# A gated linear attention and a feed-forward block in one kernel: a new order table for all five engines

## The chip, the core and the metric

The kernel runs on one core of a Trainium2 chip. The core has five engines that run side by side, each working through its own instructions in order: TensorE (PE in the profile: matrix products, PEld being the load of their stationary operand), VectorE (DVE), ScalarE (ACT), GpSimd (POOL) and SyncE (SP). DMA transfers are started by SP, ACT or POOL, each with a queue of its own, and are carried out by 16 DMA engines. Engines wait for one another on semaphores. Results of PE go to PSUM, which the kernel handles as eight banks; everything else is in SBUF.

The metric is the device time of one execution in microseconds (us). The kernel before took 189.69 us, the median of three runs (189.52 to 190.71).

## The reference

The first half is a recurrence over 768 steps for 4 batches of 8 heads with 48 features each, with a complex decay `a` whose magnitude is capped at 0.999. The second half normalises the 384 features of each token, multiplies by a gain, and applies two matrices with a ReLU between them, plus the residual.

```python
mag = np.sqrt(a_re * a_re + a_im * a_im)
scale = np.minimum(mag, 0.999) / (mag + 1e-06)
a_re_n, a_im_n = (a_re * scale, a_im * scale)
for t in range(S):                                   # S = 768
    new_re = ar * S_re - ai * S_im                   # ar, ai: a_re_n, a_im_n at t
    new_im = ar * S_im + ai * S_re
    S_re, S_im = (new_re + kv, new_im)               # kv: outer product of k[t] and v[t]
    y[:, :, t] = np.einsum('bhd,bhde->bhe', q[:, :, t], S_re)
...
xn = (x - mu) / np.sqrt(var + 1e-06) * g_ln          # x: y with the heads side by side
ch = np.maximum(xn @ w_ch1, 0.0) @ w_ch2             # 384 -> 1536 -> 384
return (x + ch).astype(np.float32)
```

## The kernel before

The 768 steps of a batch are cut into six chunks of 128, and two chunks make a pair, so that there are 12 pairs (P = 0 to 11, three for each batch) and 24 chunks (n = 2P and 2P+1). The recurrence is done by chunks: the logarithm of the magnitude and the angle of `a` are summed along the steps by matrix products with a triangular matrix, and q and k are scaled by the exponentials of these sums and turned by sine and cosine. Then a chunk is a masked product of q, k and v, plus q times a state that is carried from chunk to chunk. The feed-forward block of a pair follows when both of its chunks have their output.

Every step is a named operation (`g.add`, lines 160 to 162). For pair P the names are, in the order of their dependence:

- `are`, `aim`, `q`, `k`, `vf`: loads; `ln`, `iv`, `r`, `r2`, `u`, `l`, `lc`: logarithm of the magnitude and the ratio of the two parts of `a` (lines 454 to 475); `dec`: the sums of the logarithms on PE (line 483); `en`, `e`: their exponentials on ACT (line 487); `th`, `ph`, `car`, `sin`, `qt` or `abs`, `cos`: angle, its sums on PE (line 508), the carry to the next pair, sine and cosine.
- `ke`, `qe`, `ks`, `qs`: the scaled and turned k and q, all of them `tensor_tensor` operations recorded at line 295, on DVE or POOL.
- `kT`, `qT` (eight transposes each on PE, line 614) with `ksT`, `qsT` (the copy out of PSUM by DVE or ACT, lines 290 and 292); or `ksT`, `qsT` on SP alone, which is a DMA that transposes (line 619) and needs no PE.
- `am`, `atm`: the product of k and q and its mask (lines 637 and 295); `gm`, `G`: the carried state; `y`, `x`: output of the chunk and its copy; `bn`, `rstd`: mean and variance, and the reciprocal root, on POOL or ACT; `xtr`, `xT`: the transpose of x, three on PE (line 708) and a copy.
- `mm1.P.g.part`: the first matrix, six products of 256 columns each (line 742); `relu.P.g` (lines 759 on ACT, 761 on DVE); `mm2.n.g`: the second matrix, four products of 384 columns (line 774), for the last chunk in two halves of 192 columns; `oa` and `ot`: scaling and residual, as one DVE operation (line 790) or one on ACT and one on POOL (lines 780 and 787); `st`: the store (line 797).
- `wl`: loads of the two weight matrices through POOL's queue, with a change of type; `wp`, `wc`: gain and mean folded into the first matrix (lines 390 and 394).
- `warm.i`: fill-ins on PE (line 807), products whose result nobody reads; `tab`: loads of ACT's function tables (line 812).

What runs where and in which order is written out by hand in one string, `PLAN`. A token `relu.4.1:A4` says: operation, engine (P, A, V, G, S for PE, ACT, DVE, POOL, SP) and, where the result passes through PSUM, the bank. `@x` after a POOL operation makes its first instruction wait for the last one of `x`. `Graph.run` goes through the tokens once and emits them; each engine gets its operations in the order of the string, and the waits between engines come from the tiles and banks that the operations share:

```python
for op in steps:
    for n in op.needs:
        assert n in done or n not in planned, (op.name, n)
    ...
    op.emit()
    made[op.name] = list(traced[n_traced:])
    done.add(op.name)
for op in steps:
    if op.behind:
        tc.add_manual_dep(made[op.name][0], made[op.behind][-1].name, info,
                          reason="turns at the shared port")
```

Two things follow that the steps of the prediction use. A DMA whose letter is `A` is started by ACT's own instruction stream, in its place between the activations; one with `S` stands in SP's stream (`ring`, line 285). And a DMA's start can have to wait: the program counts DMAs with a handful of semaphores, which are used again and again, so that a start can stand until an earlier DMA, of another queue even, has landed.

Of the kernel before, what the change touches and what calls it, by code (L numbers as in the profile page):

```python
# [39 lines left out]
aim.0.0:A tab.log.0:A aim.0.1:A ue:G are.0.0:S are.0.1:S pad.e.1:G uth:V pickf:V one:G warm.0:P0 pad.ks.0:G warm.1:P0  # L40
warm.2:P0 pick:G warm.3:P0 are.1.0:S warm.4:P0 warm.5:P0 warm.6:P0 k.0.1:S ln.0.0:A warm.7:P0 car0.1:G warm.8:P0
cmean:G iv.0.0:A warm.9:P0 ident:G warm.10:P0 warm.11:P0 r.0.0:V warm.12:P0 warm.13:P0 warm.14:P0 aim.1.0:S warm.15:P0
warm.16:P0 warm.17:P0 ln.0.1:A warm.18:P0 warm.19:P0 r2.0.0:A warm.20:P0 k.0.0:S warm.21:P0 warm.22:P0 warm.23:P0
warm.24:P0 u.0.0:A warm.25:P0 warm.26:P0 warm.27:P0 warm.28:P0 iv.0.1:A warm.29:P0 l.0.0:V warm.30:P0 are.2.0:S
warm.31:P0 warm.32:P0 ln.1.0:A warm.33:P0 warm.34:P0 r.0.1:G warm.35:P0 lc.0.0:V warm.36:P0 warm.37:P0 aim.2.0:S
warm.38:P0 warm.39:P0 warm.40:P0 iv.1.0:A warm.41:P0 warm.42:P0 pad.ks.1:G warm.43:P0 warm.44:P0 warm.45:P0 warm.46:P0
warm.47:P0 zdec:G r2.0.1:A warm.48:P0 pad.e.0:G warm.49:P0 pad.qs.0:G warm.50:P0 q.0.1:S warm.51:P0 warm.52:P0 u.0.1:A
warm.53:P0 warm.54:P0 r.1.0:V warm.55:P0 dec.0.0:P0 warm.56:P1 warm.57:P1 q.1.0:S e.0.0:A0 warm.58:P1 warm.59:P1
warm.60:P1 r2.1.0:V warm.61:P1 en.0.0:A0 warm.62:P1 warm.63:P1 warm.64:P1 l.0.1:V warm.65:P1 u.1.0:A warm.66:P1
warm.67:P1 warm.68:P1 warm.69:P1 lc.0.1:V warm.70:P1 are.3.0:S warm.71:P1 warm.72:P1 warm.73:P1 ln.2.0:A warm.74:P1  # L50
l.1.0:V warm.75:P1 warm.76:P1 warm.77:P1 warm.78:P1 dec.0.1:P6 q.1.1:S warm.79:P0 warm.80:P0 lc.1.0:V en.0.1:A6
# [792 lines left out]
```

## Time and profile before

| what | value |
|---|---|
| median of three runs | 189.69 us |
| the profiled execution's own time | 190.44 us |
| its span, first to last instruction | 188.7 us |
| PE busy | 177.6 us (94%) |
| ACT busy | 159.0 us (84%) |
| DVE busy | 156.6 us (83%) |
| POOL busy | 105.0 us (56%) |
| packets of SP's DMA queue | 72.8% of 16 engines' span |
| packets of ACT's DMA queue | 17.4% |
| packets of POOL's DMA queue | 8.2% |

Busy times are of the profiled execution, and the 1.74 us between its span and its own time lie around the program. Products on PE overlap, so that their durations add up to more than they cost in sequence; what a group costs is read from starts that follow one another, or from the chain of waits, where overlaps are taken out. Starting a DMA, waiting on a semaphore and branching are not counted as busy.

### The profile page before, as it was taken

What the parts mean: (1) busy time and instruction counts of PE and PEld (TensorE: products, weight loads), DVE (VectorE), ACT (ScalarE), POOL (GpSimd) and SP (SyncE); (2) the same over time, 40 slices, a digit from 0 to 9 for tenths busy, and PEclk for the clock granted to TensorE, in tenths of its full rate; (3) what the DMA queues carried; (4) which work ended last, traced back from release to release, by engine and by line L of the source; (5) the groups of instructions that cost most, each with busy time, mean ns of one, the idle gap of its engine ahead of it and who ended that gap; (6) DMA issues with size and microseconds to landing.
All of it is one profiled execution on the core that took longest, in us unless ns stands there. A gap on an engine that the chain in (4) does not pass through costs nothing.

```text
span 188.7 us, 5157 instructions
## 1 busy us (share of the span) xinstructions
PE 177.6 (94%) x2045; PEld 136.7 (72%) x2045; DVE 156.6 (83%) x287; ACT 159.0 (84%) x224; POOL 105.0 (56%) x124
## 2 busy tenths in 40 slices
PE   5999789999999999999959999999999999998991
PEld 3897565888657888766747687878867777786781
DVE  2677999999999999999996988998989867775532
ACT  3969899999999999899959999998999979762340
POOL 7409233579187899080549392348784963940130
PEclk9999999999999999999999999999999999999998
DMA  6999999999969998889999999999799979994032
GB/s 162 287 258 179 220 213 203 222 221 193 238 119 300 184 227 232 156 194 237 161 269 210 191 239 235 281 225 201 137 170 250 216 124 178 248 218 148 5 125 83
DMA packets 133080, 37.57 MB, mean 199 GB/s; under 512 B 127168, under 2 KB 133056, under 8 KB 133056
## 3 DMA queue, kind: packets, MB, share of 16 engines
q1 hardware_dynamic: 107760, 27.21, 72.8%
q10 hardware_dynamic: 22512, 7.67, 17.4%
q0 software_dynamic: 2784, 2.36, 8.2%
q8 instruction: 16, 0.26, 0.6%
q14 instruction: 8, 0.07, 0.1%
HBM read 28.31 MB, written 4.72 MB: 175 GB/s over the span
## 4 chain that ended last, share of the span: by engine, by line
PE 57%; DVE 17%; DMA 7%; SPq 6%; ACT 3%; issue 3%; POOL 3%; ACTq 1%; DVEq 0%; POOLq 0%
PE banks L774 21%; PE banks L742 15%; PE banks L637 4%; DMA w2b<-in_moe_w_ch_dram 4%; SPq L451 4%; PE banks L508 3%; PE banks L614 3%; DVE w1b L394 3%; DMA q<-in_q_dram 3%; PE banks L483 2%; DVE atm L295 2%; SPq L410 2%; PE banks L687 2%; PE banks L690 2%; PE banks L665 2%
## 5 line engine op out<-in xcount | busy, mean ns | idle before, releaser
L774 PE MATMUL banks<-w2b,h 128*128 128x384 bf16 (+1 forms) x300 | 55.5, 319 | 0.7 <-ACT h L759 0.5
L742 PE MATMUL banks<-xT,w1b 128*128 128x256 bf16 x432 | 50.7, 272 | 0.2 <-ACT sh L551 0.2
L742 PEld LDWEIGHTS <-w1b 128*128 128x128 bf16 x432 | 41.4, 98 | 6.3 <-DVE xT L292 0.4
L774 PEld LDWEIGHTS <-h 128*128 128x128 bf16 x300 | 26.7, 97 | 13.6 <-ACT h L759 1.0
L295 DVE TENSOR_TENSOR atm<-banks,mask 128x1024 bf16<-128x1024 f32 x24 | 28.9, 1220 | 3.0 <-PE banks L637 2.2
L759 ACT ACTIVATE h<-banks 128x1024 bf16<-128x1024 f32 (+1 forms) x26 | 25.6, 1008 | 3.9 <-DVE ks L295 2.3
L812 ACT ACT_TABLE_LOAD x19 | 24.4, 1283 | 1.8 <-PEq L828 1.3
L295 POOL TENSOR_TENSOR ke<-k,en 128x384 bf16<-128x384 f32 x17 | 15.4, 916 | 14.9 <-ACT en L487 4.7
L807 PE MATMUL banks<-u_e 128*128 128x256 f16 x134 | 18.2, 293 | 2.2 <-POOL u_e L324 2.2
L787 POOL TENSOR_TENSOR ot<-ot,x 128x384 f32<-128x384 f32 x13 | 12.1, 936 | 14.6 <-ACT ot L780 12.4
L295 POOL TENSOR_TENSOR r<-aim,are 128x768 f16<-128x768 f32 (+1 forms) x8 | 13.7, 1715 | 10.8 <-DVE w1b L394 4.1
L295 POOL TENSOR_TENSOR qs<-qe,trig 128x768 bf16<-128x768 bf16 x8 | 13.0, 1640 | 8.4 <-DVE w1b L394 5.4
L807 PEld LDWEIGHTS <-u_e 128*128 128x128 f16 x134 | 13.9, 105 | 4.8 <-POOL u_e L324 1.9
L637 PE MATMUL banks<-qsT,ksT 128*128 128x128 bf16 x192 | 14.5, 219 | 2.5 <-DVE stats L700 1.9
L637 PEld LDWEIGHTS <-ksT 128*128 128x128 bf16 x192 | 12.0, 97 | 4.6 <-issue 2.3
L761 DVE TENSOR_SCALAR h<-banks 128x1024 bf16<-128x1024 f32 (+1 forms) x11 | 12.8, 1167 | 2.8 <-PE banks L742 2.8
L295 POOL TENSOR_TENSOR qe<-q,e 128x384 bf16<-128x384 f32 x12 | 10.9, 916 | 6.8 <-DVE r L295 3.6
L472 DVE SCALAR_TENSOR_TENSOR l<-r,w 128x768 f16<-128x768 f16 (+1 forms) x13 | 12.7, 977 | 1.7 <-ACT r L468 1.7
L700 DVE BATCH_NORM_STATS2 stats<-x 128x6 f32<-128x384 bf16 x24 | 13.1, 546 | 0.1
L454 ACT ACTIVATE w<-are 128x768 f32<-128x768 f32 (+1 forms) x13 | 10.4, 801 | 2.0 <-DMA are<-in_a_re_dram 1.5
L687 PE MATMUL banks<-v,atm 128*128 128x48 bf16 x192 | 11.9, 183 | 0.0
L687 PEld LDWEIGHTS <-atm 128*128 128x128 bf16 x192 | 10.7, 96 | 1.1 <-DVE atm L295 0.4
(101 smaller groups left out, 379.3 us busy)
## 6 DMA issues: line engine op xcount, KB each, us to landing
k<-in_k_dram SPq DMA_DIRECT2D x24, 192.0 KB, 5.0
q<-in_q_dram SPq DMA_DIRECT2D x24, 192.0 KB, 4.5
are<-in_a_re_dram SPq DMA_DIRECT2D x11, 384.0 KB, 5.4
aim<-in_a_im_dram SPq DMA_DIRECT2D x11, 384.0 KB, 4.9
out_dram<-ot ACTq DMA_DIRECT2D x19, 192.0 KB, 3.4
vf<-in_v_dram ACTq DMA_DIRECT2D x18, 192.0 KB, 4.7
w1b<-in_moe_w_ch_dram POOLq DMA_DIRECT2D x3, 384.0 KB, 7.0
vf<-in_v_dram SPq DMA_DIRECT2D x6, 192.0 KB, 6.6
```

Source lines behind the costliest of these rows:

```text
L295: {"DVE": nc.vector, "POOL": nc.gpsimd}[eng(name)].tensor_tensor(**kw)
L472: nc.vector.scalar_tensor_tensor(out=S_("l"), in0=S_("r2"), scalar=0.5, in1=S_("w"), op0=ALU.mult, op1=ALU.add)
L637: nc.tensor.matmul(ps[:, h], lhsT=T("ksT", n)[:, h], rhs=T("qsT", n)[:, h], start=True, stop=True)
L687: nc.tensor.matmul(ps[:, h], lhsT=T("atm", n)[:, h], rhs=T("v", P)[:, c, h], start=True, stop=nfirst)
L700: nc.vector.bn_stats(out=T("stats", n), in_=T("x", n))
L742: nc.tensor.matmul(ps[:, jj], lhsT=w1b[:, dc, ts(gi * JG + jj, C)], rhs=T("xT", P)[:, dc].rearrange("p c t -> p (c t)"), start=(dc == 0), ...
L759: act(out=dst, in_=src, func=AF.Relu)
L761: nc.vector.tensor_scalar(out=dst, in0=src, scalar1=0.0, scalar2=None, op0=ALU.max)
L774: nc.tensor.matmul(bank(own)[:, 0:w], lhsT=T("h", P)[:, j, ts(c, C)], rhs=w2b[:, j, es], start=(j == 0), stop=(j == NJ - 1))
L787: nc.gpsimd.tensor_tensor(out=T("ot", n)[:, es], in0=T("ot", n)[:, es], in1=T("x", n)[:, es], op=ALU.add)
L807: g.add(f"warm.{i}", lambda i=i: nc.tensor.matmul(bank(f"warm.{i}")[:, 0:256], lhsT=u_e[:, 0, 0], rhs=u_e[:, 1].rearrange("p j t -> p (j t ...
L812: g.add(f"tab.{nm}.{i}", lambda tab=tab: nc.scalar.preload_act_table_set(tab))
```

## The change

The string `PLAN` is replaced as a whole, and the number of fill-ins goes from 134 to 124. The code of the operations is the same. Compared by operation:

- From PE to DMA: `qT.6` (eight transposes) and `xtr.11` (three) are gone; `qsT.6` and `xT.11` are transposing DMAs on SP.
- To POOL: 5 more `ks`, 4 more `ke`, 4 more `v`, 2 more `qe`, 1 more `qs`; from POOL 5 `ot`, 1 `r`, 1 `r2`, 1 `rstd`.
- To ACT: 4 more `xT`, 2 more `x`, 2 more `r2`, 2 more `car`, 1 more `ksT`, 1 more `rstd`; from ACT 5 `oa`, 4 `v`, 3 `G`, 3 `abs`, 2 `relu`.
- DVE gets 5 `ot`, 3 `G`, 3 `abs`, 2 `relu`, 1 `r` and gives 5 `ks`, 5 `xT`, 4 `ke`, 2 `x`, 2 `qe`, 2 `car` and one each of `qs`, `ksT`, `qsT` and `r2`.
- DMA starts: 9 `vf` and 10 `st` move from ACT's stream to SP's, one `are` from SP's to ACT's. ACT's stream starts 21 DMAs where it started 39.
- The order on every engine, the banks, and the POOL operations with an `@` are new.

Of the diff (all of `PLAN`, 104 lines each way), the lines that the prediction speaks of:

```diff
-aim.0.0:A tab.log.0:A aim.0.1:A ue:G are.0.0:S are.0.1:S pad.e.1:G uth:V pickf:V one:G warm.0:P0 pad.ks.0:G warm.1:P0
...
-warm.31:P0 warm.32:P0 ln.1.0:A warm.33:P0 warm.34:P0 r.0.1:G warm.35:P0 lc.0.0:V warm.36:P0 warm.37:P0 aim.2.0:S
...
-lc.7.0:V aim.8.0:S v.5:V mm1.4.2.1:P2 relu.4.1:A4 st.3:A relu.4.0:V6 qs.6.0.1:G@v.5 kT.11:P1 relu.4.2:A2 aim.9.0:S
-dec.7.0:P4 ksT.11:V1 k.7.1:S mm2.8.0:P6 e.7.0:A4 ke.6.0.0:V am.11:P2 en.7.0:A4 ks.6.0.0:V mm2.8.1:P6 q.7.1:S bn.9:V
...
-relu.10.0:V2 mm1.10.2.0:P4 ot.19:G mm1.10.1.0:P6 relu.10.2:A4 st.18:A st.15:A st.12:A gm.22:P1 mm1.10.1.1:P6 rstd.10:A
...
-relu.11.2.0:V4 mm2.22.1:P6 mm2.23.1.0:P7 mm2.23.0.1:P0 mm2.23.1.1:P0 mm2.22.2:P6 ot.22:V6 mm2.23.2.0:P7 mm2.23.2.1:P0
-st.22:S ot.23.0:V7 st.23.0:S ot.23.1:V0 st.23.1:S
+pickf:V ue:G aim.0.0:A are.0.1:A cmean:G pick:G aim.0.1:A are.0.0:S tab.log.0:A ln.0.0:A iv.0.0:A r.0.0:V gln:S
+are.1.0:S q.0.1:S ln.0.1:A iv.0.1:A r2.0.0:A u.0.0:A r.0.1:V r2.0.1:G ident:G car0.1:G uth:V l.0.0:V lc.0.0:V
+aim.1.0:S pad.ks.0:G@lc.0.0 are.2.0:S aim.2.0:S pad.e.0:G ln.1.0:A iv.1.0:A r.1.0:V u.0.1:A one:G k.0.0:S l.0.1:V
...
+mm2.9.0:P7 ks.6.0.1:V am.11:P2 st.4:S mm2.8.0:P6 mm2.8.1:P6 r.8.0:G@qs.6.0.1 st.3:S e.7.0:A4 ke.7.0.0:G am.10:P0
...
+rstd.4:G@r2.8.0 mm2.9.1:P7 ke.7.0.1:G ot.8:V6 xtr.10:P2 ph.9.0:P0 xT.11:S are.10.0:S r2.9.0:V mm2.9.2:P7 xT.10:A2
...
+rstd.10:G@qs.11.0.0 ot.21:V1 mm1.11.2.0:P2 st.17:A mm1.11.2.1:P2 ot.20:V0 st.20:S ot.18:G@v.11 relu.11.0:A4
+mm2.23.0.1:P0 mm2.22.0:P5 relu.11.1:V6 rstd.11:G relu.11.2.0:V2 st.18:S mm2.22.1:P5 relu.11.2.1:V2 mm2.22.2:P5
+ot.22:V5 st.22:S mm2.23.1.1:P0 mm2.23.2.1:P0 ot.23.1:V0 st.21:A st.23.1:S mm2.23.0.0:P6 mm2.23.1.0:P6 mm2.23.2.0:P6
+ot.23.0:V6 st.23.0:A
...
-    for i in range(134):
+    for i in range(124):
```

In the new string the order of tokens of different engines says nothing of time, since all 43 first fill-ins, for instance, stand behind operations that they don't wait for; only the order within an engine counts.

192 lines of the change are left out of this document (95 added, 97 removed).

## The prediction

> **What bounds the kernel now.** I read the busy shares first, then the busy time by stretch, then the chain of waits, and then the order of time around each place where PE stands still.
>
> ```profile
> span 188.7 us, 5157 instructions
> PE 177.6 (94%) x2045; PEld 136.7 (72%) x2045; DVE 156.6 (83%) x287; ACT 159.0 (84%) x224; POOL 105.0 (56%) x124
> PEclk9999999999999999999999999999999999999998
> L807 PE MATMUL banks<-u_e 128*128 128x256 f16 x134 | 18.2, 293 | 2.2 <-POOL u_e L324 2.2
> ```
>
> PE is busy for 94% of the span, and its clock is granted in full. But 18.2 us of that are fill-ins (line 807), so the share doesn't say that PE is the bound at the start. So the span is cut where the first product with the first weight matrix begins (36.84 us, pair 0), and where pair 5's begins (107.45 us):
>
> ```profile
> 36.84 0.82 PE L742 MATMUL banks<-xT,w1b 128*128 128x256 bf16 x6
> 107.45 0.82 PE L742 MATMUL banks<-xT,w1b 128*128 128x256 bf16 x6
> 36.84:107.45 70.61, 68.56 (x817) 51.73 (x813) 66.95 (x122) 65.83 (x88) 45.92 (x47) 1.00 1.09 211
> 107.45:184.40 76.95, 76.27 (x897) 59.70 (x896) 59.37 (x108) 61.79 (x90) 42.28 (x40) 1.00 0.92 184
> 0.00:36.30 36.30, 31.65 (x324) 24.45 (x325) 28.46 (x56) 30.85 (x48) 16.27 (x38) 1.00 1.03 219
> 36.30:106.62 70.32, 68.27 (x821) 51.95 (x819) 66.64 (x122) 65.54 (x86) 46.46 (x47) 1.00 1.07 211
> ```
>
> The columns are the stretch, its length, and then busy time of PE, PEld, DVE, ACT and POOL. Between the two marks PE is idle for 70.61 - 68.56 = 2.05 us, and from 107.45 to 184.40 for 0.68 us. So after 36.84 us PE sets the time, with DVE and ACT close behind: the last two rows end at ACT's copies `xT.0` (36.30) and just ahead of `xT.10` (106.62), and between these ACT is idle for 70.32 - 65.54 = 4.78 us, DVE for 3.68 us. Nearly all of PE's 2.05 us is one stop:
>
> ```profile
> 94.57 1.00 ACT L759 ACTIVATE h<-banks 128x1024 bf16<-128x1024 f32 x1
> 97.45 0.36 ACTq L797 DMA_DIRECT2D out_dram<-ot  x1
> 97.92 1.02 ACT L759 ACTIVATE h<-banks 128x1024 bf16<-128x1024 f32 x1 [2.34 <-DVE ks L295]
> 98.99 0.61 PE L637 MATMUL banks<-qsT,ksT 128*128 128x128 bf16 x8 [1.91 <-DVE stats L700]
> ```
>
> The chain of waits names DVE here. But PE's product (`am.11`, banks 2 and 3) starts 0.05 us after the ReLU on ACT that empties these banks (`relu.4.2`, 97.92 + 1.02), and that ReLU starts right behind a store's start on ACT (`st.3`, 97.45 + 0.36). ACT stood 2.34 us with a store at the head of its stream. The second stop, and the end:
>
> ```profile
> 168.74 2.28 ACTq L797 DMA_DIRECT2D out_dram<-ot  x3
> 171.06 0.20 ACT L724 ACTIVATE rstd<-mv 128x2 f32<-128x2 f32 x1 [1.36 <-DVE G L292]
> 172.47 0.82 PE L774 MATMUL banks<-w2b,h 128*128 128x384 bf16 x4 [0.53 <-ACT h L759]
> 184.39 1.27 DVE L790 SCALAR_TENSOR_TENSOR ot<-banks,rstd,x 128x384 f32<-128x384 f32 x3 [2.17 <-PE banks L774]
> 185.04 1.30 SPq L797 DMA_DIRECT2D out_dram<-ot  x3
> ```
>
> Again three stores on ACT, a late `rstd.10`, a late ReLU, and 0.53 us of PE. Behind the last product come three DVE operations and three stores one after the other.
>
> **The change part by part.** The sum is made against the span of 188.7 us. The profiled execution took 190.44 us, the median is 189.69; differences are carried over as they are.
>
> Start, up to `xT.0`. PE fills time with fill-ins here, so ACT's stream decides.
>
> ```profile
> 7.55 2.12 DVE L475 TENSOR_SCALAR l<-l 128x384 f16<-128x384 f16 x1
> 11.63 0.26 DVE L475 TENSOR_SCALAR l<-l 128x384 f16<-128x384 f16 x1
> 7.42 1.00 POOL L295 TENSOR_TENSOR r<-aim,are 128x384 f16<-128x384 f32 x1 [2.76 <-ACT are L456]
> 10.84 0.49 ACT L487 ACTIVATE e<-banks 128x384 bf16<-128x384 f32 x1 [0.93 <-PE banks L483]
> 13.68 0.49 ACT L487 ACTIVATE en<-banks 128x384 bf16<-128x384 f32 x1 [0.51 <-PE banks L483]
> 21.12 0.87 ACT L534 ACTIVATE trig<-banks 128x384 bf16<-128x384 int16 x2 [0.58 <-DVE car L529]
> L464 ACT ACTIVATE r<-r 128x768 f16<-128x768 f16 x2 | 1.7, 840 | 0.2 <-issue 0.2
> L526 ACT ACTIVATE car<-banks 32x384 f16<-32x384 int16 x4 | 1.9, 484 | 0.2 <-issue 0.2
> L290 ACT CAST G<-banks 128x384 bf16<-128x384 f32 x8 | 3.8, 479 | 0.0
> L418 ACT CAST v<-vf 128x768 bf16<-128x768 f32 x4 | 3.3, 834 | 0.0
> ```
>
> `lc.0.0` took 2.12 us where its twin took 0.26, while POOL ran `r.0.1` and its fills; ACT's 0.93 us wait hangs on it. In the new table `r.0.1` is on DVE and POOL's fill stands behind `lc.0.0`, so that the 0.93 goes. Of the waits of 0.51 and 0.58 I count one as gone (0.51). ACT gets `r2.1.0`, `G.0` and two `car` before `xT.0` and loses `v.0` and the half-size `r2.0.1`: 0.84 + 0.48 + 0.48 + about 0.32 (half-size `car`, estimated from the 0.48) - 0.83 - 0.51 (estimated from the 0.84) = +0.78. Together 0.78 - 0.93 - 0.51 = **-0.66**. Bounds: all three waits go, -1.24; none, +0.78. The loads that the new order puts later (`k.0.0`, `k.0.1`) are needed only after `en.0.0`; they are costed at nothing because ACT's stream of exponentials covers them.
>
> From pair 0 to pair 5. In this stretch ACT is given three full `r2` (2.52), four `rstd`, and a net one each of `car` (0.48), `xT` and `x`, and gives up a net three `G` (1.44), one `v` (0.83) and one `oa`; `ksT` for `qsT` and `sin` for `abs` come out even.
>
> ```profile
> L725 ACT ACTIVATE rstd<-rstd 128x2 f32<-128x2 f32 x5 | 1.0, 203 | 0.2
> L724 ACT ACTIVATE rstd<-mv 128x2 f32<-128x2 f32 x5 | 1.0, 199 | 1.8 <-DVE G L292 1.4 <-DVE mv L701 0.5
> L290 ACT COPY xT<-banks 128x384 bf16<-128x384 bf16 x8 | 3.8, 481 | 5.3 <-PE banks L708 5.2
> L290 ACT CAST x<-banks 128x384 bf16<-128x384 f32 x12 | 5.7, 477 | 1.7 <-PE banks L690 1.5
> L780 ACT ACTIVATE ot<-banks,rstd 128x384 f32<-128x384 f32 x13 | 7.4, 578 | 1.3 <-PE banks L774 0.7 <-DMA out_dram<-ot 0.5
> ```
>
> That is 2.52 + 4 x 0.40 + 0.48 + 0.48 + 0.48 - 1.44 - 0.83 - 0.58 = +2.7 us, and ACT needs 65.54 + 2.7 = 68.2 us of the 70.32. `st.3` goes to SP, and its 2.34 us with it. What stays of the other 4.78 - 2.34 = 2.44 us of waits decides. All gone: 68.2, or -2.1, which is also PE's floor here (-2.05). All stay: +0.3. Half: **-0.85**, which I take. The upper bound has a stop like that of `st.3` as well: +2.7. DVE is relieved of `ke`, `ks` and `xT` here.
>
> ```profile
> 45.67 8.18 DMA w2b<-in_moe_w_ch_dram
> 55.36 0.45 PE banks L614 x8
> 176.05 0.39 PE banks L708 x6
> ```
>
> The last load of the second matrix is on the chain of waits, 8.18 us long up to 53.85. But PE's idle time in this stretch without the big stop is 2.05 - 1.91 = 0.14 us, so a better place for this load is worth 0.14 at most, and it is costed at nothing.
>
> The eleven transposes that leave PE (0.45 + half of 0.39 = 0.65 us by the chain of waits) count for nothing, because ACT holds PE in this stretch. The four fill-ins placed after the first products would take back most of it anyway (18.2 us for 134 is 0.136 each).
>
> From pair 5 on, `rstd.10` is on POOL and fewer stores are on ACT: the 0.53 us goes, **-0.5** (bounds 0 and -0.68, all of PE's idle time).
>
> Stops by DMA starts. After the start ACT's stream had 37 DMAs, and two of them cost PE 1.91 + 0.53 = 2.44 us, or 0.066 each. The new table has 17, so I add 17 x 0.066 = **+1.1** wherever they fall (bounds 0 and +2.44).
>
> End. The new table finishes `ot.22` and the half `ot.23.1` while PE works on the last half, so that one DVE operation of the three (0.42 of 1.27 us) and one store are left: **-0.85** (bound 0, if these are held up).
>
> SP's stream gets 19 stores and loads and two transposes, and gives one load. A store there waits for its `ot` with everything behind it: behind `st.9`, which waits for POOL, stand `ksT.18` and `qsT.19`, for which PE's `am.18` and `am.19` wait. The forecast charges nothing for that, since these transposes are started some products ahead of their use; if that cover goes, it is the second rival. The new `@` waits hold POOL alone, which is idle for 70.32 - 46.46 us of the stretch above. Sum: -0.66 - 0.85 - 0.5 + 1.1 - 0.85 = **-1.8**, a span of 186.9 us and a median of **187.9 us**.
>
> **The rivals.**
>
> *ACT becomes the bound (slower).* The new table gives ACT 2.7 us more between pair 0 and pair 5. If the waits at the start stay (+0.78), and the waits in the stretch stay with one blocked DMA among them (+2.7), then -0.5 and -0.85 are all that is gained: 188.7 + 2.1, or a median of 191.8 us. It decides from the point where ACT's idle time between `xT.0` and `xT.10` exceeds 2.1 us; it was 4.78. For it speaks that ACT's waits on PE and DVE were spread over the stretch, against it that half of them had one cause, which goes.
>
> *SP's queue becomes the bound.* `xT.11` is now a DMA behind other DMAs.
>
> ```profile
> ksT<-ks SPq DMA_TRANSPOSE x14, 4.4
> vf<-in_v_dram SPq DMA_DIRECT2D x6, 192.0 KB, 6.6
> q1 hardware_dynamic: 107760, 27.21, 72.8%
> ```
>
> A transposing DMA lands 4.4 us after its start, where a copy takes 0.48. Were SP 2 us behind at two such places, pair 5's products and a late `am` would wait, +2.4 us against the forecast after cover: 190.3 us. Against it: SP's queue has ends of idle time in the trace, but its packets fill 72.8% already.
>
> *PE alone sets the time (faster).* All of PE's idle time goes (-2.05 - 0.68), the start and end as above, and no DMA blocks: -4.2, or 185.5 us.
>
> *DVE loses to POOL.* POOL gets 16 elementwise operations that read SBUF and gives seven. The row of 2.12 against 0.26 us is one such meeting, 1.86 us. DVE's 3.68 us of idle time pay for two; two more would make it 191.6 us. The `@` waits speak against it.
>
> The Trainium skill, page "SBUF — State Buffer", section "Who interferes with whom", has a rule for this: GpSimd and a VectorE operation in a two-port mode take one port pair for a whole instruction, and the second fully blocks. The 2.12 us row agrees with it. By the rule each such meeting that the table doesn't order costs a whole instruction.
>
> **How the numbers follow.** A measurement of this kernel tells about 1% from no change, so faster is below 187.8 and slower above 191.6 us. Chances: forecast 0.34 (187.9, half of it under 187.8), PE alone 0.17, ACT 0.25 (three quarters above 191.6), SP 0.14 (a third above), DVE and POOL 0.10 (most of it above). Faster 0.17 + 0.17 = 0.34; slower 0.19 + 0.05 + 0.07 = 0.31; within 1%: 0.35. Range 185.5 to 192.3: from PE alone to a little above the slower cases. The forecast's own range is 186.5 to 189.5.
>
> **What would show it.** Right: no ACT store ahead of PE's product at about 97 us, ACT idle for less than 2.8 us between its first `xT` copy and pair 5's, `lc.0.0` near 0.3 us, one DVE operation behind the last product. Wrong: an idle PE before `mm1.5` released by ACT (the table asks too much of ACT), by a DMA (SP's queue), or DVE operations of 2 us beside POOL (the port). I would be most wrong if a DMA start blocked ACT in a place where the new table has no slack.

## The result, and the profile after

The changed kernel takes 199.49 us (median of four runs, 198.47 to 200.05), the kernel before beside it 189.91 us: a ratio of 1.049, with a 95% interval of 1.043 to 1.055. It is slower by 9.6 us where 1.8 us of gain were forecast, and outside the range. The profiled execution took 199.13 us. Its page:

```profile
span 196.9 us, 5119 instructions
PE 179.1 (91%) x2022; PEld 136.6 (69%) x2024; DVE 158.1 (80%) x277; ACT 155.2 (79%) x220; POOL 115.7 (59%) x131
PEclk9999999999999889999999999999999999999999
```

The span grew by 8.2 us while ACT's busy time fell from 159.0 to 155.2 us, so over the whole span the loss is not added work on ACT. There is a new mark in the clock row too: in slices 14 and 15 (64 to 74 us) PE's granted clock is below full. By stretch (columns as in the prediction), cut at the first products of pairs 0 and 5, and for ACT at `xT.0` and `xT.10`:

```profile
37.84:114.25 76.41, 70.35 (x808) 53.04 (x806) 65.52 (x109) 68.04 (x97) 51.45 (x45) 0.98 0.95 190
114.25:193.75 79.50, 77.42 (x900) 59.98 (x900) 65.80 (x114) 54.75 (x75) 42.02 (x43) 1.00 0.90 184
...
37.38:113.47 76.09, 70.31 (x815) 53.40 (x813) 65.74 (x110) 67.70 (x96) 51.88 (x46) 0.98 0.96 191
```

First mm1 comes 1.0 us late (37.84 against 36.84). From there to pair 5 it takes 76.41 us against 70.61, so 5.8 are lost. For the rest the end of the last product is the mark. In the kernel before that is 184.95, not the 184.40 at which the prediction cut:

```profile
107.45:184.95 77.50, 76.82 (x901) 60.02 (x899) 59.92 (x109) 61.79 (x90) 42.28 (x40) 1.00 0.91 183
```

In the changed kernel it is 193.77. So from pair 5 to the last product it is 79.52 against 77.50, 2.0 lost; and behind that 3.1 against 3.75, 0.6 won. The largest part lies in the first stretch, where PE is idle for 6.06 us (it was 2.05), 4.0 more. The other 1.8 is busy time, 70.35 us against 68.56; in the trace PE's clock is granted at 0.50 from 67.36 to 70.77, and 3.4 us at half the clock account for about 1.7 of it. What PE waited for there and later (all waits between 36 and 194 us; total, times, longest):

```profile
PE banks L637 <- DVE atm L295: 3.1, 1, 3.1
PE banks L742 <- ACT xT L290: 1.6, 1, 1.6
PE banks L687 <- DVE atm L295: 1.1, 1, 1.1
PE banks L742 <- DVE xT L292: 0.7, 1, 0.7
PE banks L742 <- DVE sh L553: 0.7, 1, 0.7
PE banks L742 <- DVE h L761: 0.6, 1, 0.6
PE banks L742 <- DMA xT<-x: 0.3, 1, 0.3
```

The old stop behind `st.3` at 97 us is gone, as forecast. In its place stand several others, and the longest shows the pattern. The timeline of ACT, DVE and PE around it, and behind it the same work in the kernel before (`atm.4`, `am.5`, `sin.4.0` and `car.4.0`):

```profile
62.91 0.79 ACT L551 ACTIVATE sh<-banks 128x768 f16<-128x768 int16 x1
63.72 1.28 ACT L812 ACT_TABLE_LOAD   x1
65.02 0.81 ACT L534 ACTIVATE trig<-banks 128x768 bf16<-128x768 int16 x1
...
61.73 0.68 DVE L292 COPY qsT<-banks 128x1024 bf16<-128x1024 bf16 x1
65.86 0.56 DVE L529 TENSOR_SCALAR car<-banks 32x384 f16<-32x384 int16 x1 [3.45 <-ACT trig L534]
66.45 1.22 DVE L295 TENSOR_TENSOR atm<-banks,mask 128x1024 bf16<-128x1024 f32 x1
...
63.77 0.81 PE L774 MATMUL banks<-w2b,h 128*128 128x384 bf16 x4
67.73 1.01 PE L637 MATMUL banks<-qsT,ksT 128*128 128x128 bf16 x8 [3.15 <-DVE atm L295]
```

```profile
60.11 1.22 DVE L295 TENSOR_TENSOR atm<-banks,mask 128x1024 bf16<-128x1024 f32 x1
61.82 0.61 PE L637 MATMUL banks<-qsT,ksT 128*128 128x128 bf16 x8
61.84 0.81 ACT L534 ACTIVATE trig<-banks 128x768 bf16<-128x768 int16 x1
62.66 0.48 ACT L526 ACTIVATE car<-banks 32x384 f16<-32x384 int16 x1
```

`abs.4.0` (line 551), `sin.4.0` (534) and `car.4.0` (529) all read the sums of `ph.4.0` in one pair of banks. In the kernel before all three are ACT's, and `atm.4` waits for none of them. In the new table the first two are ACT's, with a table load of 1.28 us between them, and the third is DVE's, and stands behind `sin.4.0` in the string. `car.4.0` uses nothing of `sin.4.0`, both only read, and still it starts 0.03 us after `sin.4.0` ends. DVE stands 3.45 us with `atm.4` behind it, and PE stands for `atm.4`, since `am.5` goes to its banks. The Trainium skill, page "PSUM — Partial Sum Buffer", section "PSUM bank collisions raise a hardware error", states the rule: two engines must not touch the same 32 partitions of one bank at a time, reads with reads included, so that the compiler's scheduler puts a dependence between them. This trace agrees, at a price of 3.45 us of DVE's time. The stop of 1.6 us at 48.0 is the same the other way round: `car.3.0` on ACT stood 1.55 us for `abs.3.0` on DVE, with `xT.3` behind it:

```profile
46.98 0.48 ACT L526 ACTIVATE car<-banks 32x384 f16<-32x384 int16 x1 [1.55 <-DVE sh L553]
```

And the 0.7 before 166.1 is `abs.11.0` on DVE, which had stood 1.46 us for `sin.11.0` on ACT, in banks that PE needed next.

So the theory to test is **H**: the loss comes from hand-offs between ACT and DVE at one phase bank. Its rivals are **L**, ACT's load (the prediction's first rival, whose sign did appear: ACT is idle for 76.09 - 67.70 = 8.4 us between `xT.0` and `xT.10`, far above the 2.1 from which it was to decide), **D**, the port shared by DVE and POOL, and **Q**, SP's queue.

### The profile page after: what moved, and what is told of

Read it like the earlier page. It is cut to its first block, busy times and chain, and to the rows that moved or that the text cites. A ratio compares the mean times of both kernels' runs of the same rounds, so it can differ in the third digit from the quotient of the medians.

```text
span 196.9 us, 5119 instructions
## 1 busy us (share of the span) xinstructions
PE 179.1 (91%) x2022; PEld 136.6 (69%) x2024; DVE 158.1 (80%) x277; ACT 155.2 (79%) x220; POOL 115.7 (59%) x131
## 4 chain that ended last, share of the span: by engine, by line
PE 57%; ACT 20%; DVE 10%; DMA 6%; issue 3%; SPq 1%; ACTq 1%; POOL 1%; DVEq 0%
PE banks L742 17%; PE banks L774 17%; PE banks L637 4%; ACT L812 4%; PE banks L508 4%; DMA aim<-in_a_im_dram 3%; DMA q<-in_q_dram 3%; PE banks L614 3%; PE banks L483 3%; DVE atm L295 2%; ACT e L487 2%; ACT en L487 2%; PE banks L687 2%; ACT trig L534 2%; ACT w L454 2%
## 5 line engine op out<-in xcount | busy, mean ns | idle before, releaser
L759 ACT ACTIVATE h<-banks 128x1024 bf16<-128x1024 f32 x24 | 24.3, 1020 | 11.5 <-PE banks L742 9.7
L295 POOL TENSOR_TENSOR ke<-k,en 128x384 bf16<-128x384 f32 x21 | 19.7, 945 | 14.1 <-ACT en L487 7.5
L295 POOL TENSOR_TENSOR ks<-ke,trig 128x768 bf16<-128x768 bf16 x10 | 17.0, 1702 | 3.7 <-PE banks L742 2.8
L295 POOL TENSOR_TENSOR qs<-qe,trig 128x768 bf16<-128x768 bf16 (+1 forms) x9 | 14.7, 1638 | 5.6 <-ACT trig L545 3.1
L295 POOL TENSOR_TENSOR qe<-q,e 128x384 bf16<-128x384 f32 x14 | 13.5, 975 | 7.6 <-DVE ks L295 5.4
L761 DVE TENSOR_SCALAR h<-banks 128x1024 bf16<-128x1024 f32 (+1 forms) x13 | 14.7, 1133 | 3.2 <-PE banks L742 3.1
L295 POOL TENSOR_TENSOR r<-aim,are 128x768 f16<-128x768 f32 x7 | 12.7, 1812 | 6.1 <-issue 4.7
L807 PEld LDWEIGHTS <-u_e 128*128 128x128 f16 x124 | 12.7, 105 | 4.6 <-POOL u_e L324 1.9
L295 POOL TENSOR_TENSOR r<-r 128x768 f16<-128x768 f16 (+1 forms) x4 | 5.5, 1369 | 15.7 <-DVE r L295 15.2
L295 DVE TENSOR_TENSOR qs<-qe,trig 128x768 bf16<-128x768 bf16 (+1 forms) x17 | 10.9, 644 | 2.7 <-ACT trig L534 1.5
```

The costliest lines, as they stand in the source:

```text
L295: {"DVE": nc.vector, "POOL": nc.gpsimd}[eng(name)].tensor_tensor(**kw)
L759: act(out=dst, in_=src, func=AF.Relu)
L761: nc.vector.tensor_scalar(out=dst, in0=src, scalar1=0.0, scalar2=None, op0=ALU.max)
L807: g.add(f"warm.{i}", lambda i=i: nc.tensor.matmul(bank(f"warm.{i}")[:, 0:256], lhsT=u_e[:, 0, 0], rhs=u_e[:, 1].rearrange("p j t -> p (j t ...
```

## The experiments

Ratios are to the kernel before, run on the same chip beside each; the interval is at 95%.

### Hand-offs: one engine, or another order

All readers of a bank on one engine:

```diff
-abs.3.0:V0  car.4.0:V6  abs.6.0:V2  car.9.0:V0  abs.10.0:V2  abs.11.0:V4
+abs.3.0:A0  car.4.0:A6  abs.6.0:A2  car.9.0:A0  abs.10.0:A2  abs.11.0:A4
```

> The changed kernel with all readers of one phase bank on one engine: abs.3.0, abs.6.0, abs.10.0, abs.11.0, car.4.0 and car.9.0 go from VectorE to ScalarE, at their places in the table. Theory H (hand-offs): the stops of PE at 48.0 (1.7 us), 67.7 (3.3 us, and about 1.5 us of lowered clock behind it) and 166.1 (0.9 us) are waits between engines that read the same phase bank one after the other; without the change of engine they go, less what 4.1 us more work on ScalarE takes back (four absolute values of 0.8 and two carries of 0.45, 2.5 us of it before pair 5): 193 to 196 us. Theory L (ScalarE is simply overloaded, the rival of the prediction that was priced at 191.8): more work there makes it worse: 200 to 203 us.

Every operation on its engine, four tokens elsewhere:

```diff
-abs.3.0:V0 xT.2:A2 ... car.3.0:A0
+car.3.0:A0 abs.3.0:V0 xT.2:A2 ...
-sin.4.0:A6 qsT.6:S am.4:P4 car.4.0:V6 atm.4:V4 ... atm.5:V4
+sin.4.0:A6 qsT.6:S am.4:P4 atm.4:V4 ... atm.5:V4 car.4.0:V6
-sin.9.0:A0 car.9.0:V0 ... bn.10:V
+sin.9.0:A0 ... bn.10:V car.9.0:V0
-tab.trig.17:A sin.11.0:A4 ... abs.11.0:V4
+abs.11.0:V4 tab.trig.17:A sin.11.0:A4 ...
```

> The changed kernel with every operation on its engine, only four tokens moved: car.3.0 ahead of abs.3.0, car.4.0 behind atm.5, car.9.0 behind bn.10, abs.11.0 ahead of the table load tab.trig.17. Theory H: the three long stops go because no engine stands for another's read of the phase bank: 193 to 196 us. Theory L: no work has moved between engines, so 199 to 200 us as before the edit.

And `car.4.0` alone behind `atm.5`:

> The changed kernel with one token moved: car.4.0, on VectorE as in the change, behind atm.5 instead of ahead of atm.4. Theory H in parts: this one hand-off is the stop of 3.3 us at 67.7 and the lowered clock behind it (1.5 us in that trace, up to 3 with the stops that followed when the clock alone was kept up), so 4.8 to 6 us of the 6 that all four tokens gave: ratio 1.015 to 1.025 to the kernel before. Rival: each of the four tokens gives its own stop, this one 3.3: ratio 1.03.

Measured: one engine 193.46 us, ratio 1.013 (1.008 to 1.018); four tokens 193.56 us, 1.014 (1.005 to 1.023); `car.4.0` alone 194.8 us, 1.020 (1.015 to 1.026). From 1.049 that is about 6.9, 6.7 and 5.5 us, worked out with 190 us for the kernel before. Both ways of taking the hand-offs away give the same, although one puts 3.7 us more work on ACT (its busy time is 158.9 us, it was 155.2) and the other none. So H holds and L falls as the main cause. One token is worth some 5.5 us, more than its stop of 3.15.

### The clock behind a stop

```diff
+warm.124:P0 ... warm.147:P0
 am.5:P4
-    for i in range(124):
+    for i in range(148):
```

> The changed kernel with 24 more fill-in products ahead of am.5, in the stop of 3.3 us before 67.7 (24 x 0.109 us = 2.6 us of work, less than the stop). If the lowered clock of 67.7 to 72 us (0.50 and 0.81) is a consequence of PE standing still, the clock stays at 1.0 and the time falls by about 1.5 us to 198.0 although the stop stays. If the clock falls for another reason, 199.5, or a little more where the fill-ins last longer than the stop.

Measured: 196.89 us, ratio 1.032 (1.025 to 1.038): 24 products that nobody reads make the kernel faster, by about 3.3 us by the two ratios and by 2.2 between the two profiled executions. The windows around the stop; the first number behind the five busy times is the granted clock. First the changed kernel, then the one with the fill-ins:

```profile
64.30:67.70 3.40, 0.28 (x2) 0.06 (x1) 1.81 (x3) 1.52 (x2) 0.00 (x0) 0.95 1.19 278
67.70:70.00 2.30, 2.27 (x31) 2.27 (x31) 2.13 (x4) 0.00 (x0) 1.72 (x1) 0.50 1.17 260
70.00:72.00 2.00, 2.00 (x35) 1.52 (x33) 1.35 (x4) 1.36 (x3) 2.00 (x3) 0.81 1.02 197
```

```profile
64.30:67.70 3.40, 2.87 (x27) 2.36 (x26) 1.86 (x3) 1.46 (x2) 0.00 (x0) 1.00 1.12 266
67.70:70.00 2.30, 2.30 (x41) 1.93 (x41) 2.30 (x4) 0.48 (x1) 1.78 (x1) 1.00 0.80 156
```

Kept busy, PE goes on at the full clock: 41 products in 2.30 us where 31 were done. The mean granted clock of the whole execution tells the same for all that were timed: 0.983 to 0.991 in the four of the changed kernel, 0.997 to 1.000 in the four with the fill-ins. I expected 1.5 us from that (half of 2.3 and a fifth of 2.0); pair 2's first mm1 came 1.24 us earlier (73.11 against 74.35), so that part was sized right. The rest of the 3.3 is gained later (two of the stops further on, at 94.9 and 118.3, are not there in this run, one at 112.9 is longer), and is not traced.

### The reverse, in the kernel before

```diff
-atm.4:V4 ... tab.trig.7:A ... am.5:P4 sin.4.0:A6 ... car.4.0:A6 ... abs.4.0:A6
+abs.4.0:A6 tab.trig.7:A ... sin.4.0:A6 car.4.0:V6 atm.4:V4 am.5:P4
```

> The reverse test, in the kernel before: abs.4.0 goes ahead of the table load tab.trig.7, car.4.0 to VectorE right behind sin.4.0, and atm.4 and am.5 behind car.4.0, as in the changed kernel; TensorE's own order stays. Theory H: VectorE stands until sin.4.0 ends at 63.5, atm.4 ends at 65.3 instead of 61.3, am.5 waits for it by about 3.5 us, and the clock falls behind the stop by another 1.5 us: 194 to 196 us. If other work takes up such a stop (the stop of 1.9 us at 97 us shrinks or goes): 191.5 to 193. Theory L (no work is added to ScalarE, 0.5 us is taken from it): 190 us.

Measured: 195.14 us, ratio 1.023 (1.016 to 1.029). Windows of this kernel:

```profile
61.20:64.75 3.55, 0.20 (x9) 0.12 (x5) 1.93 (x3) 1.56 (x2) 0.12 (x1) 0.99 0.93 176
64.75:67.00 2.25, 2.25 (x32) 2.25 (x33) 1.52 (x2) 0.56 (x2) 1.80 (x2) 0.50 0.83 158
```

The same hand-off, put into a kernel that had none there, makes a like stop (3.35 us) and the same half clock, and costs 4.3 us. The mean granted clock is 0.988 to 0.991 in all four executions. Theory L expected nothing of it.

### The shared port, and the transposing transfer behind it

`ks.5.0.1` takes its turn, on top of the four tokens:

```diff
-ks.5.0.1:G
+ks.5.0.1:G@qs.5.0.1
```

> The kernel with the four tokens in another order, and ks.5.0.1 on GpSimd made to take its turn behind qs.5.0.1 of VectorE, so that the two do not run side by side. Theory D (shared port): qs.5.0.1 takes 0.55 us instead of 1.98, the stop of PE at 90.0 (1.1 us) goes and the time falls by 1 us. Rival: what waits there is only the queue of VectorE, ot.4 and l.7.0 or the products of pair 5 take the stop over, and the time stays within 0.3 us.

Then `xT.11` on PE and DVE again:

```diff
-xtr.10:P2 ph.9.0:P0 xT.11:S
+xtr.11:P1 xT.11:V1 mm2.9.1:P7 ... xtr.10:P2 ph.9.0:P0
```

> The kernel with the four tokens and the turn of ks.5.0.1, and xT.11 back on TensorE's transposes and a copy by VectorE (+0.3 us on each) instead of SP's queue. Theory Q (SP's transposing transfer, 5.0 us from issue to landing, sets pair 5): the stop of 1.7 us at 109.7 goes and the gain of the turn comes through, 1.4 to 1.7 us: ratio 1.002 to 1.004 to the kernel before. Rival: the next late thing (xT.10 on ScalarE, ended 108.1) keeps pair 5 within 0.5 us of 109.7: ratio 1.008 to 1.011.

Rows of the changed kernel (DVE, POOL), and of the one with the turn:

```profile
91.74 2.01 DVE L295 TENSOR_TENSOR qs<-qe,trig 128x768 bf16<-128x768 bf16 x1
...
91.69 1.64 POOL L295 TENSOR_TENSOR ks<-ke,trig 128x768 bf16<-128x768 bf16 x1
```

```profile
86.81 0.55 DVE L295 TENSOR_TENSOR qs<-qe,trig 128x768 bf16<-128x768 bf16 x1
```

What PE waits for in the kernel with the turn, the longest first:

```profile
PE banks L742 <- DMA xT<-x: 1.7, 1, 1.7
```

Measured with the turn: 192.78 us, 1.011 (1.006 to 1.016), not told apart from the 1.014 without it. The mechanism is there (2.01 us beside POOL, 0.55 alone, and the stop of 1.1 us goes), but the time doesn't follow: PE now arrives earlier at pair 5 and waits 1.7 us for `xT.11`, whose transfer lands 5.0 us after its issue. Moving that too gives 191.97 us, 1.0045 (1.0008 to 1.008), near what theory Q expected, and pair 5 comes at 108.61 instead of 109.72. But the intervals of the three kernels overlap, and their profiled executions take 192.19 (four tokens), 192.71 and 192.18 us, so that a gain of the two steps together is not shown. By the traces pair 5 comes 0.6 us earlier than with the four tokens alone (109.20), and pair 9 1.0 us later (157.46 against 156.44). What PE waits for then, the longest:

```profile
PE banks L637 <- DMA ksT<-ks: 1.5, 1, 1.5
```

The next is again a transposing transfer, `ksT.19`, issued at 147.47 behind two loads on SP's queue and landed at 153.05.

### The start

The loads as before:

```diff
-are.0.1:A cmean:G pick:G aim.0.1:A are.0.0:S tab.log.0:A ... gln:S ... k.0.0:S
+cmean:G pick:G tab.log.0:A aim.0.1:A are.0.0:S are.0.1:S ... k.0.0:S gln:S
```

> The changed kernel with the start's transfers as in the kernel before: are.0.1 back on SP's queue, the first table load between ScalarE's two starts, the load of gln behind k.0.0. Theory S: the first mm1 product comes 1.0 us earlier (at 36.8 instead of 37.84) and the time falls by as much, to 198.5. Rival: the chain behind it is ScalarE's, the earlier start is used up by the stops at 48.0 and 67.7, and the time stays within 0.3 us of 199.5.

Measured: 200.55 us, about 1.05 (198.00 to 201.64, without an interval), and first mm1 at 39.33. My edit made a new wait:

```profile
13.03 0.68 DVE L381 TENSOR_SCALAR gc<-cmean,gln 128x128 bf16<-128x128 f32 x3 [2.71 <-DMA gln<-in_moe_g_ln_dram]
```

`lc.0.0` was 1.5 us earlier (8.21 against 9.72), and `wgc`, waiting for the later `gln`, took it all. Two other orders of DVE's and ACT's work there, the first on top of the four tokens:

```diff
-qs.0.1.0:G ... wc.1.0:V5 ks.0.0.1:V ... wc.1.1:V5 ... ks.0.1.0:V ... wp.0:P0 wc.0.0:V0 ... kT.1:P3 ksT.1:V3
+ks.0.0.1:V ks.0.1.0:V qs.0.1.0:V ... qsT.1:V1 wc.1.0:V5 ... qsT.0:V0 wc.1.1:V5 ... kT.1:P3 wp.0:P0 ksT.1:V3 wc.0.0:V0
```

> The kernel with the four tokens in another order, and VectorE's order before pair 0's first mm1 changed too: ks.0.0.1 and ks.0.1.0 ahead of wc.1.0 (which waited for wp.1 with them queued behind it), qs.0.1.0 on VectorE instead of GpSimd, wc.1.0 and wc.1.1 behind qsT.1 and qsT.0, and kT.1 and ksT.1 ahead of wp.0 and wc.0.0. Theory: the 1.0 us by which the changed kernel comes late to its first mm1 arises between 23 and 31 us on VectorE (ksT.1 ended 32.07 against 28.41), not from the loads: first mm1 at 36.8 and the time 1.0 us below the four-token kernel. Rival: ScalarE's chain to xT.0 (36.91) sets it and the first mm1 stays at 37.8.

and the second, which takes over most of the first's moves on DVE, on top of all up to `xT.11`:

```diff
-qt.0.0:P3 cos.0.0:A3 ... th.2.0:A ... qt.0.1:P4 ... sin.1.0:A6 ... cos.0.1:A4
+qt.0.0:P3 qt.0.1:P4 cos.0.0:A3 cos.0.1:A4 ... th.2.0:A ... sin.1.0:A6
```

> The kernel with the four tokens, the turn and xT.11 on TensorE (192.0, ratio 1.0045), and the start's order once more: qt.0.1 and cos.0.1 right behind qt.0.0 and cos.0.0 (cos.0.1 had come at 24.7 behind th.2.0 and sin.1.0, against 22.75 in the kernel before), ks.0.0.1, ks.0.1.0 and qs.0.1.0 on VectorE ahead of wc.1.0, kT.1 and ksT.1 ahead of wc.0.0, wc.1.1 behind qsT.0. Theory: the 1.0 us at the first mm1 come from cos.0.1's place and what VectorE could not do without it; first mm1 at 36.8 to 37.2 (VectorE's two stops of 0.9 and 0.7 us filled) and the ratio falls by 0.003 to 0.005, to about 1.000. Rival 1: first mm1 at 37.8 or later as in the first attempt, since am.0's bank is held by wc.0.2. Rival 2: it comes earlier, and the time does not follow, because a transfer holds a later pair.

Neither was faster than what it was built on: 194.6 us, 1.019 (1.010 to 1.028), first mm1 at 39.04; and 193.63 us, 1.015 (1.010 to 1.020), first mm1 at 39.37. In the second `cos.0.1` did move from 24.7 to 22.8, but in both `atm.0` went back to 33.6 and 33.9 (32.3 before the edit), because `am.0` takes the bank that `wc.0.2` reads last. One kernel with several of these edits (four tokens, the first of the two starts, the turn, and two operations moved on SP's queue) tells the same:

> The changed kernel with all of it: the four tokens, VectorE's order at the start, the turn of ks.5.0.1, and on SP's queue st.14 behind qsT.21 and k.11.1 beside k.11.0, so that the last transposes of the stop at 162.6 (1.0 us) start 1.1 us earlier. If the causes add up: 193.5 less 1.0, 1.1 and 1.0, so 190 to 191, about as long as the kernel before or 1 us faster by the span. If what follows each stop is late in any case: 192 to 193.5.

193.56 us, 1.013 (1.007 to 1.019): the causes don't add up. In its trace first mm1 comes at 39.01, and PE stands 2.0 us ahead of pair 5. So I took the start from the kernel before as a whole, all of its table up to pair 0's first mm1, with the mended table behind it:

> The table of the kernel before up to pair 0's first mm1 (with its 134 fill-ins), and from there the changed kernel's with the four tokens, the turn and xT.11 on TensorE (ratio 1.0045). Theory: the changed kernel's start is the rest of its loss: first mm1 at 36.8 instead of 37.8 and the ratio falls to 0.998 to 1.001. Rival 1: the later start was in the bargain, since operations brought ahead of it (pad.ks.2, v.1, wc.2.0 and ksT.2) come back behind it: first mm1 at 36.8, pair 1 no earlier than 46.9, ratio 1.003 to 1.006. Rival 2: a later wait for a transfer takes the gain, pair 1 a full microsecond earlier and the time unchanged.

Measured: 192.11 us, 1.006 (1.002 to 1.009). First mm1 comes at 37.07, pair 1's at 47.06, where it was 37.81 and 46.97. The stretch between pairs 0 and 1 in the kernel before, in the mended one, and in the spliced one:

```profile
36.84:44.43 7.59, 7.59 (x117) 6.39 (x114) 7.33 (x13) 7.27 (x11) 6.44 (x8) 1.00 1.11 207
```

```profile
37.81:46.97 9.16, 8.56 (x120) 6.88 (x118) 8.94 (x12) 8.40 (x13) 8.18 (x8) 1.00 1.18 191
```

```profile
37.07:47.06 9.99, 8.28 (x117) 6.60 (x114) 9.35 (x13) 9.21 (x14) 9.84 (x11) 1.00 1.15 185
```

Against the kernel before ACT does 1.1 and 1.9 us more there, DVE 1.6 and 2.0, and PE is idle for 0.6 and 1.7 us. So the late start is not what remains; an earlier one is used up at once. `r2.4.0` and `u.4.0`, 0.85 us each, had come to stand on ACT ahead of `xT.2` and `xT.3`; I moved them behind:

```diff
-r2.4.0:A x.3:A3 ... u.4.0:A ... xT.2:A2 ... xT.3:A2
+x.3:A3 ... xT.2:A2 ... xT.3:A2 r2.4.0:A u.4.0:A
```

> The spliced table (ratio 1.0059) with r2.4.0 and u.4.0, two operations of 0.85 us that the change had brought to ScalarE ahead of xT.2 and xT.3, moved behind xT.3. Theory L in one stretch (ScalarE is the bound between xT.0 and xT.3: busy 8.2 of 9.0 us there): pair 1 comes at 45.9 instead of 47.06 and the ratio falls by as much, to 0.999 to 1.001. Rival 1: xT.2 waits for x.2 on VectorE (ended 44.49) and pair 1 gains less than 0.5 us. Rival 2: pair 1 comes early, but l.4.0 and dec.4.0 come late behind u.4.0 and the gain is lost by pair 2: ratio 1.004 to 1.006.

Measured: 193.02 us, 1.013 (1.009 to 1.017). Pair 1 comes 0.5 us earlier (46.53), `sin.3.0` goes from 48.32 to 49.41, `dec.3.0` behind it makes PE stand 1.6 us at 50.3, and pair 2 is 1.1 us later. So theory L's forecast here (0.999 to 1.001) failed, and the course is that of rival 2, at a higher price. ACT's work in this stretch is late whichever part goes first, which speaks for its load as the limit there; but DVE has as much more to do, and no run tells the two apart.

### What the prediction wanted from the change, done alone

In the kernel before: `st.3` on SP, and the end in the new order.

```diff
-st.3:A relu.4.0:V6 ... q.7.1:S
+relu.4.0:V6 ... q.7.1:S st.3:S
-mm2.23.1.0:P7 mm2.23.0.1:P0 mm2.23.1.1:P0 mm2.22.2:P6 ot.22:V6 mm2.23.2.0:P7 mm2.23.2.1:P0 st.22:S ot.23.0:V7 st.23.0:S ot.23.1:V0 st.23.1:S
+mm2.23.0.1:P0 mm2.23.1.1:P0 mm2.22.2:P6 ot.22:V6 st.22:S mm2.23.2.1:P0 ot.23.1:V0 st.23.1:S mm2.23.1.0:P7 mm2.23.2.0:P7 ot.23.0:V7 st.23.0:A
```

> The kernel before with two things alone: st.3 behind q.7.1 on SP's queue instead of on ScalarE's, where it stood 2.3 us ahead of relu.4.2, and at the end the products of the last tile's second half ahead of the first's, so that one operation of VectorE and one store stand behind the last product, as in the changed kernel. If the prediction's two gains hold by themselves: the stop of 1.9 us at 97 goes, 1.5 to 1.9 us, and the end shortens by 0.8: ratio 0.985 to 0.988. Rival: st.3 on SP stands there as long and makes ksT.12 and its followers late, so that only the end's gain is left: ratio 0.995 to 0.997.

Measured: 190.78 us, 1.000 (0.996 to 1.004). Where pairs begin their first mm1 (us):

| kernel | pair 0 | 5 | 6 | 7 | 11 | last product ends |
|---|---|---|---|---|---|---|
| before | 36.84 | 107.45 | 118.18 | 131.03 | 176.92 | 184.95 |
| changed | 37.84 | 114.25 | 127.42 | 139.65 | 185.75 | 193.77 |
| changed, four tokens, turn, `xT.11` | 37.81 | 108.61 | 120.03 | 132.25 | 178.94 | 186.97 |
| before, `st.3` and end | 37.05 | 105.31 | 116.05 | 132.71 | 178.40 | 186.42 |
| the same, two loads earlier | 36.42 | 105.23 | 115.96 | 131.04 | 177.42 | 185.45 |
| the same, `st.8` and `ln.11.0` later | 36.85 | 105.31 | 116.05 | 129.91 | 175.06 | 183.09 |

The gain at 97 us is there, 2.1 us at pairs 5 and 6, and is lost before pair 7. DVE, and the windows of PE, in that kernel:

```profile
121.31 0.56 DVE L295 TENSOR_TENSOR qe<-q,e 128x384 bf16<-128x384 f32 x1 [0.65 <-DMA q<-in_q_dram]
123.35 0.96 DVE L295 TENSOR_TENSOR r<-aim,are 128x768 f16<-128x768 f32 x1 [1.48 <-DMA aim<-in_a_im_dram]
```

```profile
123.90:126.10 2.20, 0.10 (x5) 0.01 (x2) 2.20 (x4) 1.62 (x3) 1.71 (x2) 1.00 1.22 288
126.10:128.00 1.90, 1.90 (x29) 1.46 (x29) 1.87 (x5) 1.90 (x4) 0.85 (x2) 0.77 1.34 228
128.00:130.00 2.00, 2.00 (x23) 1.57 (x21) 1.36 (x2) 0.99 (x2) 2.00 (x3) 0.50 1.66 170
```

The engines came 2 us early and the loads `q.8.0` and `aim.10.0` did not. So these two went ahead of `ksT.14` on SP's queue:

> The kernel before with the two things of the last run, and on SP's queue the loads aim.10.0 and q.8.0 ahead of ksT.14, which stood there for 4.3 us. Theory Q: the gain at 97 was given back at 126.1, where r.10.0 waited 1.5 us for aim.10.0's landing at the head of VectorE's queue; with the load 5 us earlier the stop of 2.1 us and the clock of 0.50 to 0.86 behind it (1.6 us) go: ratio 0.980 to 0.987 to the kernel before. Rival: ksT.14 itself, now 1.2 us later, or the next load (are.11.0, aim.11.0) stops VectorE or TensorE as long: ratio 0.995 to 1.003.

Measured: 190.78 us, 1.000 (0.996 to 1.004), far from theory Q's number. That stop is gone, and pair 7 comes at 131.04, as in the kernel before. ACT's stream ahead of it:

```profile
123.28 0.84 ACT L453 ACTIVATE w<-are 128x768 f32<-128x768 f32 x1 [1.48 <-DMA are<-in_a_re_dram]
...
127.25 0.49 ACT L289 CAST x<-banks 128x384 bf16<-128x384 f32 x1
129.02 0.36 ACTq L796 DMA_DIRECT2D out_dram<-ot  x1
129.48 0.48 ACT L289 CAST x<-banks 128x384 bf16<-128x384 f32 x1 [1.74 <-DVE xT L291]
```

(This table is a line shorter, so that line numbers are lower by one.) `st.8`, at the head of ACT's stream, starts 0.02 us after `q.9.0`, a load of SP's queue, has landed (129.00), and `x.14` behind it is what PE waits for. It is `st.3` over again. Both waits removed:

```diff
-ln.11.0:A ... G.14:A2 ... st.8:A ... qsT.17:S
+G.14:A2 ln.11.0:A ... qsT.17:S st.8:S
```

> The kernel before with st.3 on SP, the other order of the end and the two earlier loads (ratio 0.9996, pair 6 at 115.96 against 118.18, pair 7 at 131.04 against 131.03), and in pair 7's stretch: st.8 on SP behind qsT.17 instead of on ScalarE, where it stood 1.3 us until q.9.0 landed at 129.0, and ln.11.0 behind G.14, where ScalarE had waited 1.5 us for are.11.0. Theory W (a chain of single waits for transfers, each taken by itself): pair 7 comes at 129.6 instead of 131.0 and the ratio is 0.990 to 0.994. Theory B (the transfers' pace is the bound there, the waits only show it): another wait for a transfer takes their place, pair 7 stays within 0.4 us of 131.0, ratio 0.997 to 1.002.

Measured: 189.28 us, ratio 0.9945 (0.9915 to 0.998). This is faster than both kernels, by about 1.0 us on the kernel before, and most of the way to what theory W expected (0.990 to 0.994): single waits, not a bound by the transfers' pace.

## Why the prediction was wrong, point by point

- **What bounds the kernel.** Right as far as it went: PE's stops set the time, and those taken away or put in moved it. What the reading left out is what a stop costs beyond its length.
- **Start, -0.66.** It came to +1.0. `lc.0.0` did come free of POOL (0.59 us instead of 2.12), but it starts at 9.72 instead of 7.55 and ends later, so that ACT's first exponential begins at 10.89 against 10.84, behind a wait of 0.69 us: the 0.93 counted as gone was not won. At `cos.0.0` (22.44 against 22.36) the two kernels are level, and the 1.0 us arises behind it. There the step that failed is "ACT's stream decides": DVE and the banks decide (`ksT.1` ended at 32.07 against 28.41). Which operation of the new order costs the 1.0 us is open, since three edits only made it worse. It matters little: with the old start the time did not fall.
- **Pair 0 to pair 5, -0.85.** It came to +5.8, of which 4.0 are more standstill of PE and about 1.7 its half clock, for which the sum had no term. Of the forecast's two parts the load was sized well: ACT's work rose from 65.54 to 67.70 us, +2.2 against +2.7 forecast. The step that failed is the waits: "All gone", "all stay" or "half" were the cases for waits that the old table had. The new table made waits of its own, 8.4 us of ACT's idle time instead of 1.2, and these came from operations that I had written off as even ("`sin` for `abs`") or as 0.48 us of load (`car`). I counted on which engine an operation runs, and not that it reads a bank in turn with operations of another engine. With the four tokens moved, ACT is idle for 71.17 - 67.80 = 3.4 us there, and with the turn and `xT.11` for 70.27 - 67.69 = 2.6, inside the 2.8 that I had named.
- **From pair 5 on, -0.5.** It came to +2.0. The 0.53 at 172 us went as forecast. PE's idle time rose from 0.68 to 2.08 us, above all by a late ReLU of DVE (0.6 at 118.3), the DMA start below (0.7 at 127.4) and a late `abs.11.0` (0.7 at 166.1): the step that failed is again that only waits of the old table were counted. The remaining 0.6 is busy time of PE, and is unexplained.
- **DMA starts on ACT, +1.1.** Right in kind. One of the 17 held ACT up:

```profile
122.24 0.38 ACTq L410 DMA_DIRECT2D vf<-in_v_dram  x1
122.73 1.02 ACT L759 ACTIVATE h<-banks 128x1024 bf16<-128x1024 f32 x1 [1.75 <-DMA q<-in_q_dram]
```

  `vf.8.0` stood until `q.8.0` had landed (122.22), `relu.5.2` behind it 1.75 us. ACT's `u.9.0` and with it DVE's `l.9.0` and the copy `xT.12` came late, and PE stood 0.7 us at 127.4. That is less than the 1.1 charged.
- **End, -0.85.** Right in kind, -0.6 in size: in the kernel before 3.75 us stood behind the last product, and not 4.30, since the first of the three DVE operations started 0.56 us before the products' end. In the changed kernel one operation of DVE and one store stand behind the last product, which ends at 193.77:

```profile
192.32 0.94 DVE L790 SCALAR_TENSOR_TENSOR ot<-banks,rstd,x 128x384 f32<-128x384 f32 x2 [1.74 <-PE banks L774]
192.97 0.81 SPq L797 DMA_DIRECT2D out_dram<-ot  x2
193.81 0.42 DVE L790 SCALAR_TENSOR_TENSOR ot<-banks,rstd,x 128x192 f32<-128x192 f32 x1 [0.54 <-PE banks L774]
194.30 0.34 ACTq L797 DMA_DIRECT2D out_dram<-ot  x1
```

- **Transposes off PE, nothing.** Right as far as the runs tell: with `xT.11` back on PE, three transposes and a copy more, the ratio is 1.0045 against 1.011, in intervals that overlap.
- **Rival "ACT becomes the bound".** Its threshold was passed four times over, and it was still not the cause of most of the loss, because idle time is no sign of load. Only between pairs 0 and 1 may its load be the limit, which is not shown.
- **Rival "SP's queue".** Named the right place (`xT.11`) and a size of 2.4 us. In the changed kernel PE waits only 0.3 us for it, since it comes late anyway; with the other stops gone it is 1.7.
- **Rival "DVE loses to POOL".** One meeting of 2.01 us beside 0.55 came as described, a stop of 1.1 us. Taken away by itself it gave nothing that can be told.
- **What would make it wrong.** "An idle PE before `mm1.5` released by ACT" was seen (1.6 us), and was put down in advance to the wrong cause, "the table asks too much of ACT".

By the runs, of the 0.049 that the change costs, 0.035 go with the four tokens (0.029 with `car.4.0` alone). With the turn and `xT.11` the ratio falls by another 0.009, but in intervals that overlap and without a gain between the profiled executions. So 0.0045 to 0.014 remain, and their cause is open; a late `ksT.19` and the stretch between pairs 0 and 1 are places where PE is seen to wait.

## What to carry to other kernels

Where operations of two engines read one PSUM bank, their order in the program was an order in time here, even between reads: put a read that nobody is waiting for behind the work that somebody waits for, or keep all readers on one engine. Price a stop of PE with the clock behind it, since a long one costs more than its length. And when one stop goes, look at once for the transfers that the earlier engines will meet: here the gain came through only when the third wait in a row was removed.

## What the runs showed of the hardware that was not expected

- After PE had been idle for 3.15 us (and 3.35 in the reverse test) its clock was granted at 0.50, for 3.4 us in each of the two traces; after the 1.91 us at 97 us in the kernel before it stayed at 1.00:

```profile
97.10:99.00 1.90, 0.01 (x1) 0.01 (x1) 1.73 (x6) 1.08 (x2) 0.29 (x1) 1.00 1.19 303
99.00:101.00 2.00, 2.00 (x25) 1.48 (x25) 1.47 (x3) 2.00 (x4) 1.83 (x3) 1.00 1.06 253
```

  The Trainium skill, page "TensorE: Matmul & The Clock Gate", "Part 1: The HAM clock gate", says that the clock halves after an idle window of about 3.4 us which runs freely. The 1.91 fits that, and the two longer stops, which are a little shorter than such a window, nearly do. The stop of 2.1 us in the kernel with `st.3` and the new end does not: from 1.0 us behind its end the clock was at 0.50, again for 3.4 us, and so it was from 0.85 us behind the stop of 2.0 us in the kernel with several edits. A stop well under 3.4 us can be dear, and whether it is changes from run to run: of twelve executions of the kernel with `st.3` and the new end, nine have a mean granted clock of 0.997 or more and three one of 0.982 to 0.991.
- Work that does nothing can pay in the middle of a kernel, not only at its start: 24 fill-ins in a stop, 2.2 us between the profiled executions and 3.3 by the ratios.
- A DMA start can wait for a transfer of another queue: `st.3` for `ksT.10`, `vf.8.0` for `q.8.0`, `st.8` for `q.9.0`. Each started 0.02 us behind the landing, and ACT stood 1.7 to 2.3 us for it.
